# Batch 1 in eleven tiles of 512 tokens and one of 384, with part of the last tile's element work moved to PSUM and GpSimd

## The chip, the cores and the metric

One core of a Trainium2 chip runs the whole program. The metric is the device time of one execution in microseconds. The engines are called as in the profile: PE (TensorE) for matrix products, DVE (VectorE), ACT (ScalarE) and POOL (GpSimd) for element work, SP for issuing DMAs.

## The reference

Two batches of 6016 tokens with 256 channels pass through three layers, in float32:

```
qn, kn = q, k divided by their norms over the tokens
a  = softmax(kn^T qn / tau)            # 256 x 256 per batch
x  = v @ a                             # 12032 x 256
x  = (sigmoid(x @ w_gate) * (x @ w_val)) @ w_out        # inner width 1536
h  = x @ w_in ;  out = (h - tanh(h)) @ w_out2           # inner width 2048
```

## The kernel before, in words

Every product is made from float32 numbers split in two float32r halves, high and low: high by high, high by low and low by high are added in PSUM, so each product costs three matmuls (`prod`, lines 415 to 421). The attention matrix of a batch is multiplied into the gated layer's weights, after which only two layers are left: the gated layer (kind 1, 12 units per token tile) and the second layer (kind 2, 16 units per tile).

The tokens of a batch are cut into 12 tiles (`token_tiles`, line 46), of 502 tokens eight times and of 500 four times in either batch, so there are 24 tiles, numbered from 0. A unit runs in three parts. `part_a` makes the product in one or two PSUM buffers of a ring of four and starts the element work (`s1_a`, `s2_a`); `part_b`, one unit later, splits the result into halves (ACT copies the high half at line 489, DVE or POOL subtracts for the low half at line 491); `part_c`, three units later (`LAG`), multiplies the halves by the next weights and adds into two PSUM banks, `y0` and `y1` for kind 1, `o0` and `o1` for kind 2. At the last unit of a tile in kind 1 the banks `y` are split into `yhl`, on which the tile's second layer starts; at the last unit in kind 2 ACT copies the banks `o` out and issues the DMA. A gated unit has 18 matmuls (12 and 6), a unit of the second layer 12 (6 and 6), so a tile has 216 and 192.

The order is written out by hand: units are sorted by a key (lines 626 to 632), so that the second layer of tile i runs between the gated units of tile i+1, and every engine takes its instructions in program order. For the last tile (23) there is no next tile, and its 16 units of the second layer run alone at the end; the last units of tile 22 also fall after the last gated unit of tile 23.

Element work of a unit of the second layer (`s2_a`, lines 458 to 474) with H the product in PSUM: ACT makes u = H², d = tanh(H), s from u, and a mask `big` from u; DVE makes d = H - d (470), u = H·u (471), s = (s + C_D)·u (472), and replaces s by d where the mask is set (473). All of u, d, s and big lie in SBUF, two buffers each. In the units that `tail` names (tile 23, and units 12 to 15 of tile 22) the low half of line 491 is made by POOL, and s of odd units lies in another pool (`yp`).

Of the kernel before, what the change touches and what calls it, by code (L numbers as in the profile page):

```python
# [8 lines left out]
F32 = mybir.dt.float32  # L9
# [4 lines left out]
AF = mybir.ActivationFunctionType  # L14
ALU = mybir.AluOpType
AX = mybir.AxisListType

P = 128
B, S, D = 2, 6016, 256
# [3 lines left out]
K1, K2 = F1 // P, F2 // P  # L23
TPB = 12
CH = 512
NM = 502
NW = 12
NO = 6
NI = 8

# weight chunks converted before the second layer starts, steps of conversion between units, steps to wait for a
# conversion with two buffers, units between a product and its use, units over which batch 1's scores are spread
NC2 = 16
PUMP = 3
WAIT = 4
LAG = 3
SIDE0, SIDE1 = 2 * (K1 + K2), 10 * (K1 + K2)

# h - tanh(h) = h * u * r(u) with u = h * h; r(u) = (C_S u + C_B)^2 + C_D up to U_MAX
U_MAX = 0.045  # L40
C_S = 0.2293950247517065
C_B = -0.29057879500195016
C_D = 0.2488973


def token_tiles():
    out = []
    for b in range(B):
        off = 0
        for n in [NM] * 8 + [NM - 2] * 4:  # L50
            out.append((b, off, b * S + off, n))
            off += n
        assert off == S
    return out
# [3 lines left out]
def attn_moe_kernel(  # L58
# [12 lines left out]
    nc = tc.nc  # L71
# [15 lines left out]
    def bank(tag, name):  # L87
        return pp.tile([P, CH], F32, tag=tag, name=name)

# [1 line left out]
    def split(hi, lo, src):  # L91
        nc.scalar.copy(hi, src)
        nc.vector.tensor_sub(lo, src, hi.bitcast(F32))  # L93

    def convert(pool, items, second, done=None, depth=4):
        """float64 bit patterns to float32 halves hi + lo, two chunks side by side; stops after each Vector instruction"""
        jobs = {}

        def load(n):
            if n < len(items):  # L100
                src, dst, name = items[n]
                raw = pool.tile([P, CH, 2], U32, tag="craw", bufs=depth, name=f"raw_{name}")
                nc.sync.dma_start(raw, src.bitcast(U32).rearrange("p (c two) -> p c two", two=2))
                jobs[n] = [raw[:, :, 0], raw[:, :, 1], dst, name, None]

        def rebias(n):
            if n in jobs:
                x = pool.tile([P, CH], U32, tag="cx", bufs=depth, name=f"x_{jobs[n][3]}")
                nc.gpsimd.tensor_scalar_mul(x.bitcast(F32), jobs[n][1].bitcast(F32), 2.0**-112)
                jobs[n][4] = x  # L110

        def halves(n):
            if n in jobs:
                _, _, dst, _, x = jobs.pop(n)
                t = dst()
                nc.scalar.copy(t[:, 0], x.bitcast(F32))
                (nc.vector if second else nc.gpsimd).tensor_sub(t[:, 1], x.bitcast(F32), t[:, 0].bitcast(F32))
                if done is not None:
                    done(n)

        def step(n, which):
            if n not in jobs:
                return False
            w0, w1, _, _, x = jobs[n]
            if which == 0:
                nc.vector.tensor_scalar(x, x, 3, 0x7FFFFFFF, op0=ALU.logical_shift_left, op1=ALU.bitwise_and)
            elif which == 1:
                nc.vector.scalar_tensor_tensor(x, w1, 0x80000000, x, op0=ALU.bitwise_and, op1=ALU.bitwise_or)
            else:
                nc.vector.scalar_tensor_tensor(x, w0, 29, x, op0=ALU.logical_shift_right, op1=ALU.bitwise_or)  # L130
                load(n + depth)
            return True

        for n in range(depth):
            load(n)
        for n in range(2):
            rebias(n)
        yield
        for n in range(0, len(items) + 2, 2):
            if depth == 2 and n:  # L140
                for m in (n - 2, n - 1):
                    halves(m)
                for m in (n, n + 1):
                    rebias(m)
                for _ in range(WAIT):
                    yield
            for m in (n, n + 1):
                if step(m, 0):
                    yield
            if depth > 2:  # L150
                for m in (n - 2, n - 1):
                    halves(m)
                for m in (n + 2, n + 3):
                    rebias(m)
            for which in (1, 2):
                for m in (n, n + 1):
                    if step(m, which):
                        yield
# [5 lines left out]
            if stream[0] is not None and next(stream[0], 1) == 1:  # L164
                stream[0] = None

# [1 line left out]
    ident = base.tile([P, P], F32, name="ident")  # L168
    ident2 = sp.tile([P, 2, P], F32, name="ident2")
    ones = base.tile([P, P], F32, name="ones")  # L170
# [1 line left out]
    c_m = base.tile([P, 1], F32, name="c_m")  # L172
# [15 lines left out]
    def new_aw(f, b):  # L188
        return base.tile([P, 2, 2, CH], F32R, tag=f"aw{f}", name=f"aw{f}_{b}")

# [1 line left out]
    wgv_t = [wp.tile([P, 2, 2, CH], F32R, name=f"wgv{f}") for f in range(NW // 2)]  # L192
    conv = []
    for f in range(NW // 2):
# [59 lines left out]
        nc.scalar.activation(s0, n2, AF.Sqrt)  # L254

    def softmax_steps(pool, S_, e, rk, rq):
        """row softmax of S * rk * rq, left in e: scaled scores, exponentials, division, transpose"""
        mx = pool.tile([P, 6], F32, name="mx", tag="mx")

        def scores():  # L260
            for c in range(2):
                nc.vector.scalar_tensor_tensor(e[:, c], S_[:, c], rk[:, c : c + 1], rq, op0=ALU.mult, op1=ALU.mult)
            nc.vector.tensor_reduce(mx[:, 0:2], e, axis=AX.X, op=ALU.max)
            nc.vector.tensor_scalar_mul(mx[:, 0:2], mx[:, 0:2], -1.0)

        def exps():
            for c in range(2):
                nc.scalar.activation(e[:, c], e[:, c], AF.Exp, bias=mx[:, c : c + 1], accum_out=mx[:, 2 + c : 3 + c])

        def normalise():  # L270
            nc.vector.tensor_scalar_add(mx[:, 4:6], mx[:, 2:4], 1e-9)
            nc.vector.reciprocal(mx[:, 4:6], mx[:, 4:6])
            for c in range(2):
                nc.vector.tensor_scalar_mul(e[:, c], e[:, c], mx[:, 4 + c : 5 + c])

        def turn():
            ps = ring("turn").rearrange("p (j i) -> p j i", j=2)
            for jc in range(2):
                for ic in range(2):
                    nc.tensor.transpose(ps[:, jc, ic * P : (ic + 1) * P], e[:, ic, jc * P : (jc + 1) * P], ident)  # L280
            return ps

        return scores, exps, normalise, turn
# [10 lines left out]
    tiles = token_tiles()  # L294
    NT = len(tiles)
# [72 lines left out]
    scores, exps, normalise, turn = softmax_steps(sp, S0, e0, rn[:, 2:4], rqs)  # L368
# [39 lines left out]
        wi_t.append(w2p.tile([P, 2, CH], F32R, name=f"wi{c}"))  # L408
        wv_t.append(w2p.tile([P, 2, CH], F32R, name=f"wv{c}"))

# [1 line left out]
    yp = None  # L412
    yps, yhl, ops, live = {}, {}, {}, {}

# [37 lines left out]
        prod(ps, n, [pair(wi_t[m // 2], (m % 2) * 2 * P + j * P) for j in range(2)], [(h[:, 0, j, :n], h[:, 1, j, :n]) for j in range(2)])  # L452
        live[2, i, m] = ps

    def tail(i, m):
        return i == NT - 1 or (i == NT - 2 and m >= 12)

    def s2_a(i, m):
        n = tiles[i][3]
        H = live[2, i, m][:, :n]  # L460
        u = m2.tile([P, NM], F32, tag="u", bufs=2, name=f"u{i}_{m}")[:, :n]
        d = m2.tile([P, NM], F32, tag="d", bufs=2, name=f"d{i}_{m}")[:, :n]
        late = tail(i, m)
        s = (yp if late and m % 2 else m2).tile([P, NM], F32, tag="s", bufs=2, name=f"s{i}_{m}")[:, :n]
        big = m2.tile([P, NM], BF16, tag="big", bufs=2, name=f"big{i}_{m}")[:, :n]
        nc.scalar.activation(u, H, AF.Square)  # L466
        nc.scalar.activation(d, H, AF.Tanh)  # L467
        nc.scalar.activation(s, u, AF.Square, scale=C_S, bias=c_b[:, 0:1])  # L468
        nc.scalar.activation(big, u, AF.Relu, bias=c_m[:, 0:1])  # L469
        nc.vector.tensor_sub(d, H, d)  # L470
        nc.vector.tensor_mul(u, H, u)  # L471
        nc.vector.scalar_tensor_tensor(s, s, C_D, u, op0=ALU.add, op1=ALU.mult)  # L472
        nc.vector.copy_predicated(s, big.bitcast(I16), d)  # L473
        live[2, i, m] = s

# [8 lines left out]
    def part_b(u):  # L484
        _, kind, i, c = u
        n = tiles[i][3]
        hl = mp.tile([P, 2, NM], F32R, tag="hl", bufs=LAG + 1, name=f"hl{kind}_{i}_{c}")
        x = live[kind, i, c][:, :n]
        nc.scalar.copy(hl[:, 0, :n], x)  # L489
        eng = nc.gpsimd if kind == 2 and tail(i, c) else nc.vector  # L490
        eng.tensor_sub(hl[:, 1, :n], x, hl[:, 0, :n].bitcast(F32))  # L491
        live[kind, i, c] = hl

# [20 lines left out]
                    nc.scalar.copy(t[:, :n], ops[i][o][:, :n])  # L514
                    nc.scalar.dma_start(outT[o * P : (o + 1) * P, pos : pos + n], t[:, :n])

# [1 line left out]
    qp, qctx, q2ctx, q1 = None, ExitStack(), ExitStack(), {}  # L518

    def side_open():  # L520
# [101 lines left out]
    side += [lambda g=g: side_inverse(g) for g in range(4)]  # L622
    side += [lambda: q1["sm"][0](), lambda: q1["sm"][1](), lambda: q1["sm"][2](), side_turn, side_halves]

# [1 line left out]
    units = []  # L626
    for i in range(NT):
        for c in range(K1):
# [5 lines left out]
    qb, qc, after, awq = [], [], [], []  # L634
    m2 = None
# [88 lines left out]
```

## Time and profile before

| what | value |
|---|---|
| median of 3 runs | 2418.13 us (2416.43 to 2421.8) |
| profiled execution, from the first to the last instruction | 2414.9 us |
| what lies around that span, by the median and the ends of the runs | 3.2 us (1.5 to 6.9) |
| PE busy | 2376.3 us, 98% of the span |
| DVE busy | 1877.5 us, 78% |
| ACT busy | 1580.6 us, 65% |
| POOL busy | 113.9 us, 5% |
| mean granted TensorE clock | 0.994 of full speed |

The profiled execution has no time of its own beside its span, so the span is set against the runs. In the rows below a time with two decimals at the head of a line is the start in microseconds from the span's start, and the number after it how long the instruction took. Engines work pipelined, so that the next instruction on an engine can start before the one before it has ended; the distance from start to start is what an instruction costs its engine in a full queue.

### The profile page before, as it was taken

The page shows a single profiled execution, that of the slowest core. Times are in us where ns is not written, and L with a number is a line of the kernel's source. Part 1 is how long each engine was busy: PE and PEld are TensorE (multiplying, and loading weights), DVE is VectorE, ACT ScalarE, POOL GpSimd, SP SyncE. Part 2 cuts the span into 40 slices and gives each one's busy share as a digit, 9 for nine tenths or more (in the row PEclk, how much of TensorE's full clock was granted, in tenths as well). Part 3 has the DMA queues.
Part 4 walks back from the last instruction along what each step waited for, and adds up shares of the span by engine and source line. Part 5 has one row for each costly group of instructions (what it writes and reads, how often), then busy time and mean ns, then how long its engine had stood idle before and what let it go on. Part 6 is the DMA issues. An engine that isn't in the chain of part 4 may idle for free.

```text
span 2414.9 us, 28741 instructions
## 1 busy us (share of the span) xinstructions
PE 2376.3 (98%) x10704; PEld 1970.7 (82%) x10704; DVE 1877.5 (78%) x2911; ACT 1580.6 (65%) x2817; POOL 113.9 (5%) x79
## 2 busy tenths in 40 slices
PE   8899999999999999999999999999999999999998
PEld 8677888888888888878888888888888888888876
DVE  7898778887888888877777677777777777777778
ACT  4456667676766667776666666666666666666677
POOL 5530000000000000000000000000000000000003
PEclk9999999999999999999999999999999999999998
DMA  8520000100101101001110000000000000000000
GB/s 300 213 101 18 27 26 18 35 27 28 34 18 35 36 17 35 22 27 35 53 35 9 9 18 9 9 18 1 18 18 1 18 18 1 18 9 9 9 1 17
DMA packets 37516, 81.53 MB, mean 34 GB/s; under 512 B 3840, under 2 KB 28416, under 8 KB 35840
## 3 DMA queue, kind: packets, MB, share of 16 engines
q1 hardware_dynamic: 29568, 61.09, 7.8%
q10 hardware_dynamic: 6912, 12.32, 1.3%
q0 software_dynamic: 896, 6.29, 0.6%
q8 instruction: 83, 1.36, 0.2%
q14 instruction: 57, 0.47, 0.1%
HBM read 61.08 MB, written 18.61 MB: 33 GB/s over the span
## 4 chain that ended last, share of the span: by engine, by line
PE 92%; DVE 5%; ACT 1%; issue 1%; DMA 1%; POOL 0%; SPq 0%; ACTq 0%; POOLq 0%; DVEq 0%
PE ps L421 11%; PE ps L420 11%; PE ps L419 11%; PE o L420 7%; PE h L420 7%; PE h L419 7%; PE o L421 7%; PE o L419 7%; PE h L421 7%; PE y L420 5%; PE y L419 5%; PE y L421 5%; DVE s L472 1%; DVE u L471 1%; DVE s L473 1%
## 5 line engine op out<-in xcount | busy, mean ns | idle before, releaser
L470 DVE TENSOR_TENSOR d<-h,d 128x502 f32<-128x502 f32 (+1 forms) x384 | 259.7, 676 | 287.5 <-ACT d L467 287.4
L421 PE MATMUL ps<-vhl,aw 128*128 128x502 f32 (+1 forms) x1152 | 451.3, 392 | 0.0
L420 PE MATMUL ps<-vhl,aw 128*128 128x502 f32 (+1 forms) x1152 | 449.5, 390 | 0.7 <-DVE vhl L93 0.7
L419 PE MATMUL ps<-vhl,aw 128*128 128x502 f32 (+1 forms) x1152 | 449.7, 390 | 0.0
L489 ACT CAST hl<-s 128x502 fp32r<-128x502 f32 (+1 forms) x384 | 234.6, 611 | 290.1 <-DVE s L473 290.1
L466 ACT ACTIVATE u<-h 128x502 f32<-128x502 f32 (+1 forms) x384 | 226.8, 591 | 296.9 <-PE h L421 296.5
L471 DVE TENSOR_TENSOR u<-h,u 128x502 f32<-128x502 f32 (+1 forms) x384 | 259.5, 676 | 114.6 <-ACT big L469 114.3
L420 PE MATMUL o<-hl,wv 128*128 128x502 f32 (+1 forms) x768 | 303.3, 395 | 7.6 <-POOL hl L491 4.3
L419 PE MATMUL o<-hl,wv 128*128 128x502 f32 (+1 forms) x768 | 300.7, 392 | 3.6 <-ACT out L514 1.8
L420 PE MATMUL h<-yhl,wi 128*128 128x502 f32 (+1 forms) x768 | 300.5, 391 | 2.4 <-DVE yhl L93 2.4
L419 PE MATMUL h<-yhl,wi 128*128 128x502 f32 (+1 forms) x768 | 300.8, 392 | 0.0
L421 PE MATMUL o<-hl,wv 128*128 128x502 f32 (+1 forms) x768 | 300.0, 391 | 0.0
L421 PE MATMUL h<-yhl,wi 128*128 128x502 f32 (+1 forms) x768 | 298.7, 389 | 0.0
L473 DVE COPY_PREDICATED s<-big,d 128x502 f32<-128x502 int16 (+1 forms) x384 | 284.4, 741 | 13.3
L472 DVE SCALAR_TENSOR_TENSOR s<-s,u 128x502 f32<-128x502 f32 (+1 forms) x384 | 274.3, 714 | 14.4
L468 ACT ACTIVATE s<-u,c_b 128x502 f32<-128x502 f32 (+1 forms) x384 | 275.2, 717 | 0.0
L469 ACT ACTIVATE big<-u,c_m 128x502 bf16<-128x502 f32 (+1 forms) x384 | 273.3, 712 | 0.0
L420 PEld LDWEIGHTS ps<-vhl,aw 128*128 128x128 f32 x1152 | 218.0, 189 | 46.4 <-DVE vhl L93 1.1
L419 PEld LDWEIGHTS ps<-vhl,aw 128*128 128x128 f32 x1152 | 217.3, 189 | 45.3 <-DVE aw L93 0.4
L421 PEld LDWEIGHTS ps<-vhl,aw 128*128 128x128 f32 x1152 | 216.9, 188 | 44.2
L443 DVE TENSOR_TENSOR sg<-ps,sg 128x502 f32<-128x502 f32 (+1 forms) x288 | 194.2, 674 | 69.0 <-PE ps L421 67.5
L442 ACT ACTIVATE sg<-ps 128x502 f32<-128x502 f32 (+1 forms) x288 | 170.3, 591 | 114.4 <-PE ps L421 103.4
(143 smaller groups left out, 3765.8 us busy)
## 6 DMA issues: line engine op xcount, KB each, us to landing
vraw<-in_vT_dram SPq DMA_DIRECT2D x16, 502.0 KB, 3.7
out_dram<-out ACTq DMA_DIRECT2D x32, 251.0 KB, 2.0
raw<-in_q_dram SPq DMA_DIRECT2D x48, 128.0 KB, 2.1
raw<-in_k_dram SPq DMA_DIRECT2D x48, 128.0 KB, 2.2
raw_wgv<-in_wgv_dram SPq DMA_DIRECT2D x12, 512.0 KB, 6.5
wgv_d<-wgv POOLq DMA_DIRECT2D x6, 1024.0 KB, 9.0
wb<-wgv_d SPq DMA_DIRECT2D x6, 1024.0 KB, 4.8
raw<-in_q_dram SPq DMA_DIRECT2D x11, 512.0 KB, 5.3
```

Source lines behind the costliest of these rows:

```text
L419: mm(ps[:, :n], wh, xh, start=first and j == 0, stop=False)
L420: mm(ps[:, :n], wh, xl, start=False, stop=False)
L421: mm(ps[:, :n], wl, xh, start=False, stop=last and j == m - 1)
L443: nc.vector.tensor_mul(sg[:, :n], V[:, :n], sg[:, :n])
L466: nc.scalar.activation(u, H, AF.Square)
L468: nc.scalar.activation(s, u, AF.Square, scale=C_S, bias=c_b[:, 0:1])
L469: nc.scalar.activation(big, u, AF.Relu, bias=c_m[:, 0:1])
L470: nc.vector.tensor_sub(d, H, d)
L471: nc.vector.tensor_mul(u, H, u)
L472: nc.vector.scalar_tensor_tensor(s, s, C_D, u, op0=ALU.add, op1=ALU.mult)
L473: nc.vector.copy_predicated(s, big.bitcast(I16), d)
L489: nc.scalar.copy(hl[:, 0, :n], x)
```

## The change

Batch 1 is cut into eleven tiles of 512 tokens and one of 384; batch 0 stays as it was. `NM`, the width of the buffers in SBUF, goes from 502 to 512. In the last tile H·u no longer overwrites u but goes to the PSUM bank `y0` or `y1` (as w), which the gated layer no longer needs, and line 472 reads it there. In odd units of the last tile the mask is made by GpSimd in place of ACT. The low halves of units 12 to 15 of tile 22, which GpSimd made, go back to DVE, and their s to the common pool.

```diff
-NM = 502
+NM = 512
...
-        for n in [NM] * 8 + [NM - 2] * 4:
+        for n in [502] * 8 + [500] * 4 if b == 0 else [NM] * 11 + [S - 11 * NM]:
...
-    def tail(i, m):
-        return i == NT - 1 or (i == NT - 2 and m >= 12)
...
-        late = tail(i, m)
-        s = (yp if late and m % 2 else m2).tile([P, NM], F32, tag="s", bufs=2, name=f"s{i}_{m}")[:, :n]
+        s = (yp if i == NT - 1 and m % 2 else m2).tile([P, NM], F32, tag="s", bufs=2, name=f"s{i}_{m}")[:, :n]
...
+        last = i == NT - 1
+        w = bank(f"y{m % 2}", f"w{m}")[:, :n] if last else u
...
-        nc.scalar.activation(big, u, AF.Relu, bias=c_m[:, 0:1])
+        if last and m % 2:
+            nc.gpsimd.tensor_scalar(big, u, U_MAX, 1.0, op0=ALU.is_gt, op1=ALU.mult)
+        else:
+            nc.scalar.activation(big, u, AF.Relu, bias=c_m[:, 0:1])
         nc.vector.tensor_sub(d, H, d)
-        nc.vector.tensor_mul(u, H, u)
-        nc.vector.scalar_tensor_tensor(s, s, C_D, u, op0=ALU.add, op1=ALU.mult)
+        nc.vector.tensor_mul(w, H, u)
+        nc.vector.scalar_tensor_tensor(s, s, C_D, w, op0=ALU.add, op1=ALU.mult)
...
-        eng = nc.gpsimd if kind == 2 and tail(i, c) else nc.vector
+        eng = nc.gpsimd if kind == 2 and i == NT - 1 else nc.vector
```

## Rows read from the trace of the kernel before

**Rows 1.** The page: busy time by engine, and the chain that ended last.

```profile
PE 2376.3 (98%) x10704; PEld 1970.7 (82%) x10704; DVE 1877.5 (78%) x2911; ACT 1580.6 (65%) x2817; POOL 113.9 (5%) x79
...
PE 92%; DVE 5%; ACT 1%; issue 1%; DMA 1%; POOL 0%; SPq 0%; ACTq 0%; POOLq 0%; DVEq 0%
```

**Rows 2.** Busy time by stretch; columns: stretch, length, each engine's busy time, PEclk, DMA.

```profile
1400.00:1600.00 200.00, 200.00 (x878) 165.40 (x877) 149.28 (x232) 131.13 (x235) 0.00 (x0) 1.00 0.04 11
...
2000.00:2200.00 200.00, 200.00 (x881) 165.65 (x880) 149.73 (x234) 130.29 (x235) 0.00 (x0) 1.00 0.03 11
...
2350.00:2380.00 30.00, 27.79 (x113) 21.88 (x112) 27.97 (x35) 25.20 (x46) 10.16 (x8) 0.94 0.05 18
2380.00:2400.00 20.00, 17.84 (x74) 12.93 (x72) 19.17 (x25) 16.64 (x30) 7.59 (x6) 1.00 0.00 0
2400.00:2415.00 15.00, 8.98 (x20) 5.25 (x18) 6.50 (x9) 5.14 (x9) 3.74 (x3) 0.56 0.09 34
```

**Rows 3.** Timeline of DVE: tile 22's last unit and the start of tile 23.

```profile
2349.26 0.66 DVE L471 TENSOR_TENSOR u<-h,u 128x500 f32<-128x500 f32 x1
2349.96 0.68 DVE L472 SCALAR_TENSOR_TENSOR s<-s,u 128x500 f32<-128x500 f32 x1
2350.67 0.74 DVE L473 COPY_PREDICATED s<-big,d 128x500 f32<-128x500 int16 x1
2351.30 0.67 DVE L470 TENSOR_TENSOR d<-h,d 128x500 f32<-128x500 f32 x1
```

**Rows 4.** Timeline of all engines: tile 23's last unit and the end.

```profile
2402.74 0.72 DVE L473 COPY_PREDICATED s<-big,d 128x500 f32<-128x500 int16 x1
...
2403.35 0.66 DVE L470 TENSOR_TENSOR d<-h,d 128x500 f32<-128x500 f32 x1
2403.49 0.61 ACT L489 CAST hl<-s 128x500 fp32r<-128x500 f32 x1 [0.54 <-DVE s L473]
...
2403.93 0.67 DVE L471 TENSOR_TENSOR u<-h,u 128x500 f32<-128x500 f32 x1
...
2404.23 1.25 POOL L491 TENSOR_TENSOR hl<-s,hl 128x500 fp32r<-128x500 f32 x1 [2.07 <-ACT hl L489]
...
2404.70 1.31 DVE L472 SCALAR_TENSOR_TENSOR s<-s,u 128x500 f32<-128x500 f32 x1
...
2406.05 0.72 DVE L473 COPY_PREDICATED s<-big,d 128x500 f32<-128x500 int16 x1
...
2408.85 0.79 PE L420 MATMUL o<-hl,wv 128*128 128x500 f32 x1 [0.44 <-POOL hl L491]
```

**Rows 5.** Groups by line on DVE from 2352 us to the end.

```profile
L472 DVE SCALAR_TENSOR_TENSOR s<-s,u 128x500 f32<-128x500 f32 x16 | 22.0, 1376 | 1.7
```

**Rows 6.** Timeline of PE: first and last of twelve 512-column groups, with the start behind each.

```profile
1133.12 0.39 PE L289 MATMUL aw<-wb,aT 128*128 128x512 f32 x1
...
1134.50 0.38 PE L419 MATMUL h<-yhl,wi 128*128 128x500 f32 x1
...
1228.82 0.39 PE L289 MATMUL aw<-wb,aT 128*128 128x512 f32 x1
...
1230.20 0.39 PE L419 MATMUL ps<-vhl,aw 128*128 128x502 f32 x1
```

**Rows 7.** Timeline of PE: first and last of six matmuls of 256 columns.

```profile
451.41 0.28 PE L223 MATMUL qk<-hl 128*128 128x256 f32 x1
...
452.00 0.28 PE L225 MATMUL qk<-hl 128*128 128x256 f32 x1
```

**Rows 8.** Timeline of PE at the start of tile 23's second layer.

```profile
2348.23 0.49 PE L420 MATMUL h<-yhl,wi 128*128 128x500 f32 x1 [2.22 <-DVE yhl L93]
```

**Rows 9.** Line 109 on POOL: one undisturbed pass; then durations in ns, min/median/max.

```profile
163.25 1.54 POOL L109 TENSOR_SCALAR x_wv<-raw_wv 128x512 f32<-128x512 f32 x1
...
L109 POOL TENSOR_SCALAR x_wo<-raw_wo x6: 1507/1732/3113, 94.0 to 109.4; 128x512 f32<-128x512 f32 x6
```

## The prediction, made before the change was run

> **What bounds the kernel now.** I read the page's shares first: PE is busy 98% of the span, and the chain that ended last lies on PE for 92% of it and on DVE for 5% [rows 1]. Then the stretches: in two long stretches of batch 1 PE is never idle, DVE is busy three quarters of the time and ACT two thirds; near the end, at 2380 to 2400 us, PE drops to 89% while DVE is at 96% [rows 2]. So there are two regimes, and the change touches both. In the long one only PE's matmuls count. In the end, where tile 23's second layer runs alone, DVE sets the pace, and the timeline shows with what. A unit that nothing disturbs costs DVE 0.70 for line 471 (2349.26 to 2349.96), 0.71 for 472, 0.63 for 473 [rows 3] and 0.58 for 470 (2403.35 to 2403.93 [rows 4]): 2.62 us. But units come 3.34 us apart there: line 472 takes 1.31 us in place of 0.68, and 1376 ns in the mean of the last 16 [rows 5]. The reason is in rows 4. POOL makes the low half of the unit before from 2404.23 to 2405.48; line 472, which reads s and u, both in SBUF, starts at 2404.70 and ends 0.53 after POOL. It waited. Lines 470 and 471 read one operand from PSUM, and 471 took its usual 0.67 although POOL began inside it. The wait closes a loop: 473 ends, ACT copies the high half, POOL subtracts, 472 waits for POOL, 473 follows.
>
> **Term 1, PE's long stretch.** Tiles, instructions and total columns stay; what moves is which columns lie in the long stretch. Start to start, a matmul of 502 columns costs 200/878 = 0.2278 us and one of 500 200/881 = 0.2270 [rows 2]; one of 256 costs 0.59/5 = 0.118 [rows 7]. The line through 256 and 500 has 0.447 ns a column: 0.1752 at 384 and 0.2324 at 512. But the trace has 512-column matmuls among PE's full queue: twelve groups of six, 1.38 us in the first and in the last, 0.2300 each [rows 6]. I take 0.231, between the two. Gated layer of batch 1 (216 matmuls a tile): 216 x (8 x 0.2278 + 4 x 0.2270) = 589.8 before, 216 x (11 x 0.231 + 0.1752) = 586.7 after: -3.1. Second layer of tiles 12 to 22 (192 a tile): 192 x (8 x 0.2278 + 3 x 0.2270) = 480.7 before, 192 x 11 x 0.231 = 487.9 after: +7.2, since 116 columns leave the last tile for the tiles ahead of it. Together **+4.1**; with 0.2300 it is -0.4, with 0.2324 +10.3. DVE and ACT grow in step with PE there and stay hidden. Wider buffers, input loads and output DMAs in batch 1 cost nothing under PE's full queue; the DMA share there is 0.03 to 0.04 [rows 2].
>
> **Term 2, the passage to tile 23.** PE idles 2.22 us there, waiting for `yhl` [rows 8], and DVE is the late one. Three low halves of tile 22 go back from POOL to DVE ahead of it or right behind, 3 x 0.58 = +1.7; two waits of line 472 there go away, each at most 0.63 (1.31 - 0.68 [rows 4]), some -1.0; wider units of tile 22 add 0.2. **+1.0**, with 0 (hidden by PE's queue) and +2 as ends. The same columns sit in `s` of the common pool with two buffers; DVE runs these units in order, so nothing new waits.
>
> **Term 3, the 16 units of tile 23.** Line 470's 0.58 us for 500 columns is at most 1.16 ns a column, so 116 columns are worth 0.13 us at most; I take 0.12 for each of the four: 0.46 for 470, 0.58 for 471, 0.59 for 472, 0.51 for 473, together 2.14 us a unit. PE needs 12 x 0.1752 = 2.10. ACT was busy 16.64 of 20 us, 2.78 a unit of 3.34 [rows 2]; by 384/500 that is 2.1, and it loses every other mask. So DVE would set the pace at 2.14, with PE right behind, if POOL disturbed nothing. Line 472 now has one operand in PSUM, as 471 had, and I take it that it no longer waits. What about 473? It reads `big` and `d`, both in SBUF. No row has it beside a busy POOL; between "does not wait", like 471, and "waits", like 472, its operands are those of 472, so I take that it waits.
>
> Walk from the start of a 473 at 0. ACT's copy starts at 0.63 (0.75 before: 2402.74 to 2403.49), POOL's subtraction at 1.25 (0.74 later before, now 0.62), and lasts 0.97 (1.25 x 384/500, rounded up), to 2.22 [rows 4]. DVE would reach the next 473 at 2.14 and waits until 2.22. The mask of the odd unit after that is queued on POOL behind this subtraction. Its price has no row: the nearest is a one-input POOL pass at 512 columns, 1.54 us undisturbed [rows 9], by columns 1.16; ends are near 0 and 3.11, the longest such pass. The waiting 473 runs first (0.51), then the mask (1.16), then the next subtraction (0.97), and the 473 after that has waited for all: 2.64. A pair costs 2.22 + 2.64 = 4.86, a unit 2.43. From the first line 470 of tile 23 (2351.30 [rows 3]) to its last (2403.35 [rows 4]) are 15 intervals, 52.05 us, of which 15 x 3.34 = 50.1 is the pace and 2.0 the start and the copying out of tile 22. After: 15 x 2.43 + 1.5 = 38.0. **-14.1**. Behind the mask only POOL's subtraction is queued, and behind that the `o` products on PE.
>
> The Trainium skill (SBUF — State Buffer, Who interferes with whom) says that a DVE instruction with two SBUF inputs and a GpSimd instruction that reads SBUF exclude each other; that agrees with the 1.31 us of line 472, and by it 473 would wait for the mask too, which speaks against this half of the change. The Trainium skill (GPSIMD Engine Reference, Performance versus the Vector engine) gives 769 ns for a tight one-input loop over 512 elements, half of the 1.54 us in the row; by that page the mask would be an estimated 0.58, the pair 2.22 + 2.14, and the sum about -14.5.
>
> **Term 4, the end.** From the last line 470 to the end were 11.5 us (2403.35 to 2414.9). Lines 470 to 472 took 2.70 and now 1.63 plus some 0.5 of waiting; behind the last 473, the 2.80 us up to PE's product with the low half (2406.05 to 2408.85) shrink by 23%, 0.65, and I allow 0.5 for the products and copies behind it. **-1.7** (-1 to -2.3). The output DMA stays.
>
> **Sum:** 4.1 + 1.0 - 14.1 - 1.7 = -10.7 us. The span goes from 2414.9 to 2404.2; the median of the runs lies 3.2 above the span, so 2407.4.
>
> PE's clock: it was granted 1.00 at 2380 to 2400 with PE 89% busy, and 0.56, partly the lower level, behind 2400 where only `o` products were left [rows 2]. At 2.1 of 2.43 us PE stays as busy as before, so I cost this at nothing; if it fell to the lower level within tile 23, 12 matmuls would take about 4 us, and PE would be the bound.
>
> **The rivals.**
> (a) 473 does not wait. Then the unit is 2.14 us, term 3 is 15 x 2.14 + 1.5 - 52.05 = -18.45 and term 4 -2.3: -15.6, **2402.5**. For it: line 471 ran beside a busy POOL undisturbed. Against: 473's operands.
> (b) The PSUM operand does not free 472, so that part of the change does nothing. 472 would come at 0.51 + 0.46 + 0.58 = 1.55 and wait until 2.22, 473 follows at 2.81: 15 x 2.81 + 1.5 - 52.05 = -8.4, sum -5.0, **2413.1**. Line 471 speaks against it.
> (c) A mask of 2.33 us (3.11 by columns): second interval 0.51 + 2.33 + 0.97 = 3.81, 3.02 a unit, sum about -1.9, **2416.2**: no difference that can be told.
> (d) The other side, one mechanism: GpSimd's mask is slow whatever its width, and 473 waits for it. At 3.11 the second interval is 4.59, the unit 3.41, term 3 +0.5, sum +3.9, **2422.0**. It decides from a mask of 2.6 us on, where the sum is 0, and shows as slower from 3.2. For it: a comparison with two constants and a bf16 output has no row on POOL. Against: the undisturbed passes take 1.54 at a greater width.
>
> **How the numbers follow.** The forecast gets 0.45, (a) 0.30, (b) 0.08, (c) 0.09, (d) 0.08. 0.2% is 4.8 us, about what a measurement of this kernel can tell from no change. The forecast with the upper end of term 1 is still -4.5, (a) is faster throughout, (b) for half of its ends: faster 0.78, within 0.2% 0.15, slower 0.07 (the upper part of (d), since nothing caps an operation without a row). The range takes the forecast with both ends of term 1 (2402.9 to 2413.6) and (b), (a) down to 2400, and reaches to the edge of (c): 2400 to 2416.
>
> **What would show it.** Line 472 in tile 23 near 0.56 us beside a busy POOL; 473 stretched where POOL works; intervals of 470 alternating near 2.2 and 2.6; the mask near 1.2 us; 512-column matmuls at 0.230 to 0.232 start to start; first line 470 of tile 23 some 5 us later than 2351.30. A mask beyond 2.6 us, a 472 that still lasts over 1 us, or PE at the lower clock within tile 23 would make it wrong.

## The result, and the profile after

The changed kernel takes 2373.14 us (median of 4 runs, 2371.08 to 2378.72) against 2418.07: a ratio of 0.9818, with a 95% interval of 0.9803 to 0.9833. That is 45 us, four times the 10.7 forecast, and below the range. The profiled execution is the slowest of the four (2378.72, span 2376.9; the other spans are 2369.3 to 2372.6), so the rows below show 38 of the 45 us.

The lines of the changed kernel stand one further down: 470 to 473 of before are 471 to 474, 491 is 492; 468 is GpSimd's mask. The page first, busy time by engine and the chain that ended last, against [rows 1]:

```profile
PE 2335.7 (98%) x10704; PEld 1959.8 (82%) x10704; DVE 1874.0 (79%) x2915; ACT 1564.9 (66%) x2809; POOL 118.9 (5%) x83
...
PE 91%; DVE 5%; ACT 1%; issue 1%; DMA 1%; POOL 0%; ACTq 0%; POOLq 0%; DVEq 0%; SPq 0%
```

The picture is the same, still 10704 matmuls and still 98%, but PE is busy for 41 us less (2376.3 to 2335.7). Stretches of the kernel after (stretch, length, busy time of PE, PEld, DVE, ACT, POOL with counts, clock, DMA), one in batch 0, two in batch 1, one in tile 23's second layer:

```profile
400.00:600.00 200.00, 200.00 (x934) 169.38 (x933) 168.63 (x266) 139.82 (x255) 0.00 (x0) 1.00 0.10 29
...
1400.00:1600.00 200.00, 200.00 (x884) 165.62 (x883) 152.72 (x233) 131.15 (x235) 0.00 (x0) 1.00 0.04 14
...
2000.00:2200.00 200.00, 200.00 (x884) 165.62 (x883) 151.35 (x232) 132.40 (x237) 0.00 (x0) 1.00 0.03 11
...
2327.00:2368.00 41.00, 36.37 (x190) 32.49 (x188) 36.69 (x64) 32.99 (x72) 28.29 (x22) 1.00 0.04 13
```

and the two of the kernel before that were not shown:

```profile
400.00:600.00 200.00, 200.00 (x916) 167.02 (x915) 164.96 (x260) 138.56 (x251) 0.00 (x0) 1.00 0.09 28
...
2351.30:2403.40 52.10, 46.31 (x183) 34.93 (x182) 49.13 (x62) 43.32 (x79) 18.99 (x15) 0.95 0.03 10
```

Two things were not forecast. In batch 1, 200 us hold 884 matmuls of 512 columns where they held 878 to 881 narrower ones [rows 2]: 0.2262 each, where 0.231 was taken. And batch 0, whose tiles did not change, fits 934 where it fitted 916. The granted clock is 1.00 in all of these long stretches, before and after, so it is not the clock. PE's timeline after, first and last of 27 matmuls in a row, against [rows 6]:

```profile
1499.91 0.39 PE L419 MATMUL ps<-vhl,aw 128*128 128x512 f32 x1
...
1505.81 0.39 PE L421 MATMUL o<-hl,wv 128*128 128x512 f32 x1
```

26 steps in 5.90 us are 0.2269. Tile 23's second layer on DVE, its passage from tile 22, against [rows 3]:

```profile
2326.63 0.68 DVE L492 TENSOR_TENSOR hl<-s,hl 128x512 fp32r<-128x512 f32 x1
2327.22 0.55 DVE L471 TENSOR_TENSOR d<-h,d 128x384 f32<-128x384 f32 x1
2327.69 0.55 DVE L472 TENSOR_TENSOR w<-h,u 128x384 f32<-128x384 f32 x1
2328.35 0.56 DVE L473 SCALAR_TENSOR_TENSOR s<-s,w 128x384 f32<-128x384 f32 x1
2329.01 0.60 DVE L474 COPY_PREDICATED s<-big,d 128x384 f32<-128x384 int16 x1
```

The low half of line 492 is DVE's again, as the diff has it. The first line 471 of tile 23 comes at 2327.22, 24 us earlier than its like before and not 5 later. PE idles there 0.88 and 1.93 us, against 2.22 in one piece [rows 8]:

```profile
2321.23 0.45 PE L419 MATMUL h<-yhl,wi 128*128 128x384 f32 x1 [0.88 <-ACT yhl L92]
2323.61 0.54 PE L420 MATMUL h<-yhl,wi 128*128 128x384 f32 x1 [1.93 <-DVE yhl L93]
```

A settled pair of units after, DVE and POOL of the timeline of all engines (ACT and PE left out but for one copy), against [rows 4]; the first line is the one mask that found nothing in its way, to be set beside [rows 9]:

```profile
2336.23 1.50 POOL L468 TENSOR_SCALAR big<-u 128x384 bf16<-128x384 f32 x1 [1.51 <-ACT u L464]
...
2345.04 1.02 POOL L492 TENSOR_TENSOR hl<-s,hl 128x384 fp32r<-128x384 f32 x1 [1.08 <-ACT hl L490]
...
2345.42 0.55 DVE L473 SCALAR_TENSOR_TENSOR s<-s,w 128x384 f32<-128x384 f32 x1
...
2346.08 0.60 DVE L474 COPY_PREDICATED s<-big,d 128x384 f32<-128x384 int16 x1
2346.14 1.85 POOL L468 TENSOR_SCALAR big<-u 128x384 bf16<-128x384 f32 x1
...
2348.07 1.00 POOL L492 TENSOR_TENSOR hl<-s,hl 128x384 fp32r<-128x384 f32 x1
...
2348.35 1.18 DVE L474 COPY_PREDICATED s<-big,d 128x384 f32<-128x384 int16 x1
```

Line 473 (472 of before) starts inside POOL's subtraction and takes 0.55: with its operand in PSUM it no longer waits. Line 474 (473 of before) does: 1.18, and it ends 0.46 after POOL, where the one before took 0.60. The subtraction it waits for was late because the mask stood ahead of it on POOL. This is the loop that the prediction walked. Groups by line on DVE in this part, against [rows 5]:

```profile
L474 DVE COPY_PREDICATED s<-big,d 128x384 f32<-128x384 int16 x16 | 14.0, 877 | 1.6
L473 DVE SCALAR_TENSOR_TENSOR s<-s,w 128x384 f32<-128x384 f32 x16 | 8.9, 555 | 1.7
```

Cut into legs at three instructions, the profiled executions compare so (us; e1, e12 and e8 are experiments below):

| leg | before | after | e1 | e12 | e8 |
|---|---|---|---|---|---|
| start to the split of `vhl` of tile 12 | 1222.3 | 1213.4 | 1205.1 | 1207.0 | 1206.1 |
| from there to the first d = H - d of tile 23 | 1129.0 | 1113.8 | 1107.5 | 1112.4 | 1113.8 |
| fifteen units, to the last d = H - d | 52.05 | 39.81 | 52.73 | 43.67 | 36.79 |
| to the end | 11.5 | 9.9 | 11.3 | 9.8 | 9.0 |

The two ends went nearly as forecast. What was missed lies in the first two legs, 24 us of this execution and some 6 more of the others. In the first leg e1, e12 and e8, which have the same batch 0, are 6 to 8 us ahead of this execution, and the traces show where it lost them. From 197.6 to 335.5 us its 591 products stand 233.3 ns apart, whatever their kind; then come six matmuls of 256 columns, and behind them the products take 223.8. In e1, e12 and e8 they take 223.3 there already. So the stretch from 200 to 400 us holds fewer matmuls after (the first line) than before (the second), with PE busy throughout and the clock at 1.00 in both:

```profile
200.00:400.00 200.00, 200.00 (x885) 166.22 (x884) 154.27 (x242) 135.29 (x243) 0.00 (x0) 1.00 0.06 19
...
200.00:400.00 200.00, 200.00 (x893) 166.05 (x892) 156.16 (x245) 135.51 (x245) 0.00 (x0) 1.00 0.07 20
```

591 products times 9.9 ns are 5.9 us. What brings PE into this slower rhythm is open.

### The profile page after: what moved, and what is told of

Same layout as the page of the kernel before. It is cut to its first block, busy times and chain, and to the rows that moved or that the text cites. A ratio compares the mean times of both kernels' runs of the same rounds, so it can differ in the third digit from the quotient of the medians.

```text
span 2376.9 us, 28760 instructions
## 1 busy us (share of the span) xinstructions
PE 2335.7 (98%) x10704; PEld 1959.8 (82%) x10704; DVE 1874.0 (79%) x2915; ACT 1564.9 (66%) x2809; POOL 118.9 (5%) x83
## 4 chain that ended last, share of the span: by engine, by line
PE 91%; DVE 5%; ACT 1%; issue 1%; DMA 1%; POOL 0%; ACTq 0%; POOLq 0%; DVEq 0%; SPq 0%
PE ps L420 11%; PE ps L419 11%; PE ps L421 11%; PE o L420 7%; PE o L421 7%; PE o L419 7%; PE h L420 7%; PE h L421 7%; PE h L419 7%; PE y L421 5%; PE y L419 5%; PE y L420 5%; DVE s L473 1%; DVE s L474 1%; DMA raw<-in_k_dram 0%
## 5 line engine op out<-in xcount | busy, mean ns | idle before, releaser
L471 DVE TENSOR_TENSOR d<-h,d 128x512 f32<-128x512 f32 (+3 forms) x384 | 260.4, 678 | 260.4 <-ACT d L465 260.3
L420 PE MATMUL ps<-vhl,aw 128*128 128x512 f32 (+3 forms) x1152 | 444.9, 386 | 0.7 <-DVE vhl L93 0.7
L419 PE MATMUL ps<-vhl,aw 128*128 128x512 f32 (+3 forms) x1152 | 445.2, 386 | 0.0
L421 PE MATMUL ps<-vhl,aw 128*128 128x512 f32 (+3 forms) x1152 | 444.6, 386 | 0.0
L472 DVE TENSOR_TENSOR u<-h,u 128x512 f32<-128x512 f32 (+2 forms) x368 | 251.4, 683 | 112.2 <-ACT big L470 111.8
L420 PE MATMUL o<-hl,wv 128*128 128x512 f32 (+3 forms) x768 | 299.3, 390 | 9.1 <-POOL hl L492 5.8
L474 DVE COPY_PREDICATED s<-big,d 128x512 f32<-128x512 int16 (+3 forms) x384 | 289.1, 753 | 14.3
L419 PE MATMUL o<-hl,wv 128*128 128x512 f32 (+3 forms) x768 | 298.0, 388 | 2.0 <-ACT hl L490 1.2
L420 PE MATMUL h<-yhl,wi 128*128 128x512 f32 (+3 forms) x768 | 297.2, 387 | 2.1 <-DVE yhl L93 2.1
L419 PE MATMUL h<-yhl,wi 128*128 128x512 f32 (+3 forms) x768 | 296.9, 387 | 0.9 <-ACT yhl L92 0.9
L421 PE MATMUL o<-hl,wv 128*128 128x512 f32 (+3 forms) x768 | 297.7, 388 | 0.0
L421 PE MATMUL h<-yhl,wi 128*128 128x512 f32 (+3 forms) x768 | 297.0, 387 | 0.0
L466 ACT ACTIVATE s<-u,c_b 128x512 f32<-128x512 f32 (+3 forms) x384 | 275.1, 716 | 3.5 <-DVE hl L492 3.5
L470 ACT ACTIVATE big<-u,c_m 128x512 bf16<-128x512 f32 (+3 forms) x376 | 268.4, 714 | 0.0
L473 DVE SCALAR_TENSOR_TENSOR s<-s,u 128x512 f32<-128x512 f32 (+2 forms) x368 | 253.1, 688 | 12.6
L492 DVE TENSOR_TENSOR hl<-s,hl 128x512 fp32r<-128x512 f32 (+2 forms) x368 | 248.4, 675 | 0.0
```

The costliest lines, as they stand in the source:

```text
L419: mm(ps[:, :n], wh, xh, start=first and j == 0, stop=False)
L420: mm(ps[:, :n], wh, xl, start=False, stop=False)
L421: mm(ps[:, :n], wl, xh, start=False, stop=last and j == m - 1)
L472: nc.vector.tensor_mul(w, H, u)
L473: nc.vector.scalar_tensor_tensor(s, s, C_D, w, op0=ALU.add, op1=ALU.mult)
```

## The experiments

All kernels compute the whole reference; they differ in tiles, buffers, padding and in who makes what. Times are medians of 4 runs (10 for e2, e3, e4 and e6) beside runs of the kernel before on the same chip (2416.9 to 2418.2). "Pitch" is the mean distance from one matmul's start to the next in the trace, over all products of a kind and width in batch 1 (1230 to 2240 us). The kinds by moving operand and weight: ps is `vhl` by `aw`, y is `hl` by `wo`, h is `yhl` by `wi`, o is `hl` by `wv`.

**e1_buffers512: the buffers alone.** The kernel before with wider buffers and nothing else.

```diff
-NM = 502
+NM = 512
...
-        for n in [NM] * 8 + [NM - 2] * 4:
+        for n in [502] * 8 + [500] * 4:
```

> The kernel before with its own tiles of 502 and 500 tokens and its own tail; only the buffers in SBUF are 512 columns wide, so that the halves of vhl, yhl and hl lie 2048 bytes apart in place of 2008. Layout theory (where a moving half starts in SBUF sets what a matmul costs): all 502- and 500-column matmuls fall from 0.228 and 0.227 us start to start to about 0.225 and 0.2245, as batch 0 of the changed kernel shows, 9800 matmuls by 2.8 ns: 25 to 33 us faster, about 2388. Width theory (only matmuls of 512 columns are cheap, the fall in batch 0 is chance): 0 to 6 us faster, 2412 to 2418.

2379.91 us, ratio 0.9844 [0.9828, 0.986]: **38 of the 45 us**, with the same 24 tiles, the same instructions and the old tail, more than the 25 to 33 that the layout theory gave. Stretches of e1 (columns as above), one in batch 0 and one in batch 1:

```profile
400.00:600.00 200.00, 200.00 (x936) 169.48 (x935) 167.00 (x264) 140.68 (x256) 0.00 (x0) 1.00 0.10 30
...
1400.00:1600.00 200.00, 200.00 (x897) 167.99 (x896) 147.99 (x230) 130.52 (x237) 0.00 (x0) 1.00 0.04 14
```

897 in place of 878: the pitch of 502 columns, 227.4 to 228.5 by kind, became 223.3 to 223.4. The program has 24 x 408 = 9792 products of all four kinds and either width. Over both batches their mean pitch fell by 4.2 ns (227.8 to 223.7 between 230 and 2240 us), and 9792 x 4.2 ns is 41 us.

**e2_skew514 and e3_buffers504: is it width or a particular width?** e2 is the kernel after with `NM = 514` and its own tiles; e3 the kernel before with `NM = 504` and its own tiles.

```diff
-NM = 512
+NM = 514
...
-        for n in [502] * 8 + [500] * 4 if b == 0 else [NM] * 11 + [S - 11 * NM]:
+        for n in [502] * 8 + [500] * 4 if b == 0 else [512] * 11 + [384]:
```

```diff
-NM = 502
+NM = 504
...
-        for n in [NM] * 8 + [NM - 2] * 4:
+        for n in [502] * 8 + [500] * 4:
```

> The changed kernel with its own tiles of 512 and 384; only the buffers are 514 columns wide, so that the halves lie 2056 bytes apart. Layout theory: 512-column matmuls go from 0.2267 back to 0.230 to 0.231, and 502 to 0.228: 18 us in batch 1 and 12 to 15 in batch 0, about 2405. Width theory: within 5 us of the changed kernel, 2371 to 2378.

> The kernel before with buffers 504 columns wide: halves 2016 bytes apart, a multiple of 32 but not of 64 bytes. Layout theory at 32 bytes: as with 512-wide buffers, about 2388. Layout theory at 64 bytes or more: half of the halves still start askew, a gain of half that or less, 2400 to 2418. Width theory: 2418.

e2: 2413.68, ratio 0.9982 [0.9973, 0.9992]; e3: 2413.08, 0.998 [0.997, 0.9989]. The change with buffers two columns wider than its own brings some 4 us: it lost more than the layout theory said (about 2405). A stretch of e2 with 512-column matmuls:

```profile
1400.00:1600.00 200.00, 200.00 (x863) 162.22 (x862) 148.45 (x227) 131.94 (x233) 0.00 (x0) 1.00 0.03 11
```

863 against 884 after: 0.2317, where the prediction had 0.231. So its durations were those of the old kind of layout, and the layout is the thing that moved.

**e4_hl_only, e5_halves512, e6_rest512: which buffers?** The kernel before (tiles and element code) with 512 columns for `hl` alone (e4), for `vhl`, `yhl` and `hl` (e5), or for all others but these (e6, which is e1 with 502 in the three).

```diff
-        hl = mp.tile([P, 2, NM], F32R, tag="hl", bufs=LAG + 1, name=f"hl{kind}_{i}_{c}")
+        hl = mp.tile([P, 2, 512], F32R, tag="hl", bufs=LAG + 1, name=f"hl{kind}_{i}_{c}")
...
-        h = vp.tile([P, 2, 2, NM], F32R, tag="vhl", name=f"vhl{i}")
+        h = vp.tile([P, 2, 2, 512], F32R, tag="vhl", name=f"vhl{i}")
...
-                h = pool.tile([P, 2, 2, NM], F32R, tag="yhl", name=f"yhl{i}")
+                h = pool.tile([P, 2, 2, 512], F32R, tag="yhl", name=f"yhl{i}")
```

The first pair is e4, all three are e5.

> The kernel before, where only the buffer hl (moving operand of the y and o matmuls, 168 of the 408 matmuls of a tile) is 512 columns wide. If a matmul pays for the start of its own operand: y and o fall by some 2.5 ns, ps and h stay, 10 to 12 us faster, about 2407. If the cost comes from elsewhere in the layout (the writes of DVE and ACT, or the matmuls' phase against each other): all kinds move alike, or none.

> The kernel before where the three buffers that PE reads as moving operands (vhl, yhl, hl) are 512 columns wide, so that all halves start 32 bytes past a multiple of 64; the buffers of the element work (u, d, s, sg, big, out) and of the input stay at 502. Own-read theory (PE pays for the starts of its moving operands, and one askew kind spoils the others, which is why hl alone brought nothing): all kinds at 0.2235 to 0.2255, 33 to 40 us faster, about 2380. Contention theory (PE's reads collide with askew accesses of ACT and DVE): no kind below 0.227, within 6 us of 2418.

> The reverse: only the buffers of the element work and of the input are 512 wide, vhl, yhl and hl stay at 502. Own-read theory: within 6 us of 2418. Contention theory: the gain of the run with all buffers at 512, about 2380.

e4 2422.2 (1.0016 [1.0006, 1.0025]), e5 2403.73 (0.9947 [0.993, 0.9963]), e6 2419.73 (1.0009 [1.0, 1.0018]). None of the parts gives the whole: with `hl` at 512 even the products that read it stayed at 228, and e5 lies between the two forecasts made for it. So width was the wrong quantity to vary; what differs as well is where the buffers lie. In e1 and in the kernel after, `vhl`, `yhl`, `hl`, both halves of each (2048 bytes apart), and all weights begin at a byte address of the partition that leaves 224 when divided by 256; before, the halves are 2008 bytes apart and scattered, and in e5 they begin at 160, 160 and 96, against weights at 224.

**e10_shift32: e1 with 32 bytes of padding** ahead of `sg`, of `hl`, of the element buffers and of the second `yhl`.

```diff
+    mp.tile([P, 8], F32, name="pad1")
...
+        if (kind, i, c) == (1, 0, 0):
+            mp.tile([P, 8], F32, name="pad2")
...
+                yp.tile([P, 8], F32, name="pad4")
...
+            m2.tile([P, 8], F32, name="pad3")
```

> The kernel before with all buffers 512 columns wide, where pads of 32 bytes put the buffers of the element work (sg, u, d, s, big, out) at a multiple of 64 while vhl, yhl and hl stay 32 bytes past one. If the element buffers must have the same place within 64 bytes as PE's operands: the gain of the 512-wide element buffers goes, 0.2265 and more start to start, about 2400 to 2404. If it is enough that each buffer's parts lie alike, or the place does not matter: 2380.

2404.11 (0.9947 [0.993, 0.9963]); y and o rose to 228, h to 225, ps stayed at 224. It looked like contention with the element buffers. That reading did not hold: the pads lay ahead of other buffers too, so `hl` had moved by 64 bytes and the second `yhl` by 128. Four more runs take these apart.

**e13 to e16: e1 with one group moved.** e13 moves `vhl`, `yhl`, `hl`, `aw`, `wo` and the element buffers by 32 bytes, but not `wi` and `wv`; e14 the element buffers alone, by 32; e15 `hl` by 64 bytes, e16 by 128, and in both `u`, `d`, `s`, `big` and `out`, which lie behind `hl`, move with it.

```diff
+    base.tile([P, 8], F32, name="pad0")
```

is e13, ahead of `wo`; e15 has the following, and e16 the same with 32 columns in either pad; e14 has pads of 8 columns ahead of `sg` and `u` and of 56 behind, so that `hl` and `yhl` keep their place.

```diff
+        if (kind, i, c) == (1, 0, 0):
+            mp.tile([P, 16], F32, name="pad2")
...
+                yp.tile([P, 48], F32, name="pad4")
```

> The tiles of 502 and 500 with buffers 512 wide (as in e1_buffers512, 2379.9 us), with 32 bytes of padding ahead of everything but the last two weights: all halves (vhl, yhl, hl), two weights (aw, wo) and the element buffers begin at 0 instead of 224 modulo 256; wi and wv, which the products of h and of o read as stationary operands, stay at 224. If what counts is that all moving operands begin at one and the same phase: 502-token products stay at about 224 ns, total 2375 to 2385 us. If the moving operand has to agree with the weight it is multiplied with: ps (weights aw) and y (wo) stay at 224, h and o rise to about 228, total 2393 to 2404 us. If phase 224 itself is the good one: all four at about 228, total 2413 to 2420 us.

> As e1_buffers512, with the element buffers (sg, u, d, s and the large ones) moved by 32 bytes, to 0 modulo 256, while every half and every weight stays at 224. If only the start of the moving operands counts: all products at about 224 ns, 2376 to 2384 us. If it is how the element buffers that the other engines read and write at the same time lie against the halves: y and o at about 228 ns as in e10_shift32, 2398 to 2408 us.

> As e1_buffers512, with hl moved by 64 bytes, to 32 modulo 256 (u, d and s come to 32 too), vhl and yhl left at 224. If the own start of the moving operand counts: the products y and o, which read hl, at about 228 ns, ps and h at 224, 2398 to 2408 us (as e10_shift32 gave, where the element buffers had moved as well). If it was the element buffers in e10_shift32: all at 224, 2376 to 2384 us.

> As e1_buffers512, with hl moved by 128 bytes, to 96 modulo 256 and thus to the same place modulo 128 as before. If a place modulo 128 (or 64 or 32) is what counts: all products at about 224 ns, 2376 to 2384 us. If modulo 256: y and o at 226.5 to 228 ns, 2390 to 2408 us.

**e17_w_shift and e18_all_192: the counter-proof.** In e17 no moving operand moves, only the weights `wi` and `wv`, by 32 bytes; in e18 everything goes to a new common place.

The first line, behind the tiles of `wi` and `wv`, is in both, the second in e18 alone.

```diff
+    w2p.tile([P, 8], F32, name="pad5")
...
+    base.tile([P, 56], F32, name="pad0")
```

> As e1_buffers512, with only the weights wi and wv moved by 32 bytes, to 192 modulo 256; every half, aw, wo and the element buffers stay at 224. No moving operand moves. If what counts is that a moving operand and the weight it is multiplied with begin at the same place modulo 256: h (yhl by wi) and o (hl by wv) at about 228 ns, ps (vhl by aw) and y (hl by wo) at about 224, total 2396 to 2408 us. If the moving operand's own place decides: all at 224, 2376 to 2384 us.

> As e1_buffers512, with every half, all four weights and the element buffers moved to 192 modulo 256. If only the agreement of moving operand and weight counts: all products at 223.5 to 225 ns, total 2376 to 2388 us. If 224 modulo 256 is a good place by itself: all at about 228 ns, 2413 to 2420 us.

Distance in bytes, modulo 256, between the start of a moving operand and that of its weight (for e5 of the first `yhl` buffer, the second is at 128), and pitch of the 502-column products of batch 1:

| run | median us | ps: distance, ns | y | h | o |
|---|---|---|---|---|---|
| e1 | 2379.9 | 0, 223.4 | 0, 223.4 | 0, 223.4 | 0, 223.3 |
| e18 | 2379.4 | 0, 223.4 | 0, 223.4 | 0, 223.4 | 0, 223.3 |
| e14 | 2380.0 | 0, 223.4 | 0, 223.5 | 0, 223.4 | 0, 223.3 |
| e13 | 2403.7 | 0, 224.4 | 0, 225.7 | 32, 227.9 | 32, 227.8 |
| e17 | 2404.2 | 0, 224.4 | 0, 225.7 | 32, 227.9 | 32, 227.8 |
| e15 | 2403.7 | 0, 224.2 | 64, 228.2 | 0, 224.2 | 64, 228.2 |
| e16 | 2398.1 | 0, 223.5 | 128, 227.6 | 0, 224.4 | 128, 227.2 |
| e5 | 2403.7 | 64, 227.1 | 128, 226.5 | 64, 227.4 | 128, 226.7 |

In e17 one and the same `hl` is multiplied with `wo`, in its old place, and with `wv`, moved by 32 bytes. PE's timeline of e17, six products h, six products o, and later six products y (its lines 420 to 422 are 419 to 421 of the kernel before):

```profile
1500.30 0.38 PE L420 MATMUL h<-yhl,wi 128*128 128x502 f32 x1
...
1501.67 0.39 PE L420 MATMUL o<-hl,wv 128*128 128x502 f32 x1
...
1503.04 0.39 PE L420 MATMUL ps<-vhl,aw 128*128 128x502 f32 x1
...
1505.72 0.39 PE L420 MATMUL y<-hl,wo 128*128 128x502 f32 x1
...
1507.06 0.38 PE L420 MATMUL ps<-vhl,aw 128*128 128x502 f32 x1
```

Six h take 1.37 us, six o 1.37, six y 1.34. And e18, all at 192, is as fast as e1. A stretch of e18:

```profile
1400.00:1600.00 200.00, 200.00 (x897) 168.01 (x896) 147.77 (x231) 130.54 (x238) 0.00 (x0) 1.00 0.04 14
```

and the same stretch of e17, 11 matmuls fewer:

```profile
1400.00:1600.00 200.00, 200.00 (x886) 166.87 (x885) 150.42 (x234) 133.32 (x239) 0.00 (x0) 1.00 0.04 14
```

So neither the place of the moving operand (e17 leaves it) nor a particular place (e18) nor the element buffers (e14) make the difference between these runs, but **whether a moving operand and its weight begin at the same place modulo 256 bytes**. Modulo 128 is not enough (e16), and modulo 512 is not needed: in e1 h and o lie 256 bytes apart modulo 512, ps and y 0, and all four take the same.

The rule is not the whole of it. The 591 products at 233.3 ns in the kernel after agree with their weights too. Kinds that agree lose 1 to 2 ns in e13 and e17 when others disagree, and their 500-column products up to 3 (ps 226.8 in e15, 223.6 in e1). In e15 that loss of the 502-column products lies at the seam: the first h or ps behind a y or o takes 228.8 to 229.8 ns (221.2 to 222.5 in e1), those inside a row of their own kind 223.4 to 223.7. And in e5 the 500-column ps had 221.7, the lowest of all.

**e12_old_tail: the tiles without the tail's edits.** The kernel after, with the element code of the kernel before, which is the kernel before with these lines:

```diff
-NM = 502
+NM = 512
...
-        for n in [NM] * 8 + [NM - 2] * 4:
+        for n in [502] * 8 + [500] * 4 if b == 0 else [NM] * 11 + [S - 11 * NM]:
```

> The changed kernel's tiles and 512-wide buffers with the whole end of the kernel before: H times u over u in SBUF, every mask on ACT, low halves of tile 22's last four units on POOL. Theory: line 472 waits for POOL again and units of 384 come 2.8 us apart (1.55 after a 473, then 0.67 of waiting), 15 x (2.8 - 2.56) = 3 to 4 us and 1 more at the passage: 2374 to 2379. Rival that all of the gain at the end is the edits and none the width of 384: 14 us slower than the changed kernel, 2387.

2374.32 (0.9822 [0.9807, 0.9836]), 1.2 us above the changed kernel and inside its interval. Line 472 waits as it did, and a settled unit takes 2.74 us. Its group on DVE:

```profile
L472 DVE SCALAR_TENSOR_TENSOR s<-s,u 128x384 f32<-128x384 f32 x14 | 15.6, 1112 | 1.5
```

In the table of legs e12 against e1 is what the tiles alone do: +4.8 us in the second leg, -9.1 in tile 23's units, -1.5 behind. The first leg has +1.9 more, but nothing differs there, and 1.7 of it is there at the first split of `vhl` already (83.2 against 81.5 us).

**e9_w_sbuf and e8_act_mask: the two halves of the tail's edit.** e9 puts w in SBUF, e8 gives all masks back to ACT.

The first edit is e9, the second e8.

```diff
-        w = bank(f"y{m % 2}", f"w{m}")[:, :n] if last else u
+        w = mp.tile([P, NM], F32, tag="sg", bufs=2, name=f"w{m}")[:, :n] if last else u
```

```diff
-        if last and m % 2:
+        if False:
```

> The changed kernel with w of the last tile in the SBUF buffers of sg in place of PSUM; the mask of odd units stays on GpSimd. Theory that the PSUM operand is what frees line 473 from POOL: 473 lasts 1.1 us and more where POOL works, the interval of units goes from 2.56 to 2.8 or 3.1 in the mean, 4 to 8 us slower than the changed kernel, 2377 to 2381. Rival that the narrower tile alone freed it: 473 stays at 0.56, no difference, 2373.

> The changed kernel with every mask on ACT, as before; w stays in PSUM. In the changed kernel's trace the pairs of units of tile 23 take 5.12 us, 2.26 and 2.86, and the mask lasts 1.85. Theory that line 474 waits for the mask on POOL: without it every interval is 2.26 or PE's and ACT's 2.1 to 2.2, 15 x 0.3 = 4 to 5 us faster than the changed kernel, about 2368.5. Rival that ACT without the masks is what gave the short intervals: 2 to 5 us slower, about 2377.

e9: 2375.53 (0.9834 [0.9818, 0.985]), between its two forecasts, so the trace decides: units of 2.75 and 2.88, fifteen in 43.26 where the kernel after takes 39.81. Groups on DVE in e9, where 473 waits again and 474 hardly does:

```profile
L473 DVE SCALAR_TENSOR_TENSOR s<-s,w 128x384 f32<-128x384 f32 x13 | 13.1, 1010 | 1.4
L474 DVE COPY_PREDICATED s<-big,d 128x384 f32<-128x384 int16 x14 | 9.7, 694 | 1.4
```

e8: 2367.40 (0.9797 [0.9782, 0.9811]); every settled unit 2.27, fifteen in 36.79. The same lines in e8, neither waiting long:

```profile
L474 DVE COPY_PREDICATED s<-big,d 128x384 f32<-128x384 int16 x16 | 10.5, 653 | 1.7
...
L473 DVE SCALAR_TENSOR_TENSOR s<-s,w 128x384 f32<-128x384 f32 x16 | 8.9, 555 | 1.7
```

Without the mask the tail's edits are worth 6.9 us in the fifteen units (43.67 in e12, 36.79 in e8), and without the PSUM operand 0.4 (43.26 in e9). GpSimd's mask gives 39.81 - 36.79 = 3.0 us away in the units and 0.9 behind them.

**e7_both and e11_both_act: better versions.** e7 cuts batch 0 as batch 1; e11 does that too and takes e8's mask.

```diff
-        for n in [502] * 8 + [500] * 4 if b == 0 else [NM] * 11 + [S - 11 * NM]:
+        for n in [NM] * 11 + [S - 11 * NM]:
```

> The changed kernel with both batches in eleven tiles of 512 and one of 384. With 0.2267 for 512 columns, 0.1752 for 384, and 0.2252 and 0.2245 for 502 and 500 as batch 0 of the changed kernel shows, batch 0 goes from 408 x (8 x 0.2252 + 4 x 0.2245) = 1101.4 to 408 x (11 x 0.2267 + 0.1752) = 1088.9: 12 us faster than the changed kernel, about 2361. If the fixed part of a matmul does not matter (cost in step with columns): no difference, 2373.

> Both batches in eleven tiles of 512 and one of 384, and every mask on ACT; w in PSUM. The two single runs gave 2367.4 each against 2373.1 for the changed kernel; if they add, 2361 to 2363. If the saving in batch 0 and the one at the end are the same time (the clock, or run-to-run phase): 2367.

e7 2367.43 (0.9796 [0.9782, 0.9811]); e11 **2362.86** (0.9775 [0.976, 0.9789]), the fastest of all, 10 us below the kernel after. e7 gained half of the 12 us forecast for it, against the kernel after: the forecast took 0.2252 and 0.2245 us for batch 0 from the one profiled execution, which had the 233.3 ns in it. With 0.2234 and 0.2237, as in e1, the same sum gives some 5. In e11 the 512-column products have a pitch of 226.7 to 226.9, so a column costs 0.443 ns, against 223.4/502 = 0.445 in e1.

## Why the prediction was wrong, by its own steps

**The step that failed** is the sentence in Term 1 that wider buffers cost nothing under PE's full queue. It asked what the wider buffers cost on queues that PE hides; it did not ask what they do to PE itself. They changed how moving operands and weights lie to each other, and every large product fell by some 4 ns: -38.2 us (e1), where 0 was put and no rival stood. The pitches of [rows 2, 6] were taken as a function of the columns alone; 0.231 for 512 is right in the old kind of layout (0.2317 in e2) and 0.2267 in the new one. With -38.2 the sum would have been -48.9; measured were -45.

**Term 1's arithmetic** held: from the split of tile 12 to tile 23's units the tiles alone cost +4.8 (e12 against e1), forecast +4.1. The start of those units itself is 6.8 later, but the other 1.9 lie in batch 0, where nothing differs. With the durations of the new layout (0.2234, 0.2237, 0.2267 and 0.1749 us for 502, 500, 512 and 384 columns) the same sum gives +3.9, since all of them fell together.

**Term 2**, +1.0: from the split of tile 12 to the first d of tile 23 the new tail takes 1.4 more than the old (1113.8 against 1112.4).

**Term 3**, -14.1, came out at -12.2. The mechanism was the one walked: 473 freed, 474 waiting for the subtraction (the prediction's 472 and 473), intervals alternating, at 2.26 and 2.86 where 2.22 and 2.64 were forecast. The mask was mis-sized: 1.50 undisturbed and 1.85 with the wait for 474, taken as 1.16 from [rows 9] by columns. So the settled pace is 2.56 and not 2.43, 1.9 us in fifteen. Most of the term is the narrower tile (-9.1, e12); the edits add -3.9, and without the mask they would add -6.9 (e8).

The Trainium skill (SBUF — State Buffer, Who interferes with whom) says that a DVE instruction with two SBUF inputs contends with a GpSimd instruction that reads SBUF, and one with at most one SBUF input, outside the two-port modes, does not. The traces agree: line 474 took 1.18 where it started behind POOL's subtraction and 0.60 where it started ahead of the mask, and for line 473 the mean is 1.01 with w in SBUF (e9) and 0.56 with w in PSUM. The Trainium skill (GPSIMD Engine Reference, Performance versus the Vector engine) gives 769 ns over 512 elements as the best case of a tight loop; the mask, at 1.50 us for 384 columns, is far from it, and the measurement decides.

**Term 4**, -1.7: measured -1.6.

**The rivals.** (a) falls: 474 waits, and 2.27 a unit needs a POOL without masks (e8). (b) falls by e9, (c) and (d) by the mask's 1.50 to 1.98 us. The clock was 1.00 from 2327.2 to 2366 us, as assumed for the settled units; at the start of tile 23's second layer it was at the lower level (0.50) for 3.4 us, from 2323.8, behind 3.8 us in which PE was busy for 1.0. The kernel before had 3.4 us of 0.50 too, from 2360.9. All rivals were about the tail, some 15 us in all, while PE's part, 92% of the chain [rows 1], got one term with a spread of 11 us. Batch 0, whose tiles don't change (the 916 that became 934), was not even in the sum.

## What to carry to other kernels

Where PE is the bound, the buffers' addresses belong to the cost of its matmuls: before a duration of the old kernel is used for a new one, see whether the change moves a matmul's operands, and try a layout in which moving operands and weights begin at the same place modulo 256 bytes (halves of 2048 bytes did it here, since everything ahead of them left the same remainder). Test a buffer's width apart from the tiles that use it, since one constant can hold the whole gain. A DVE instruction that waited for GpSimd was freed here by moving one of its inputs to PSUM, but the next one with both inputs in SBUF then took over the wait, and new work on GpSimd in the same loop made that wait longer. Look at more than one execution: the profiled one had 6 us of slower matmuls that other traces of the same batch 0 don't show.

## What the runs showed of the hardware that was not expected

The pitch of a float32r matmul in a full queue depends here on the relation of two addresses: 223.4 ns for 502 columns where moving operand and weight begin at the same place modulo 256 bytes, 226.5 to 228.2 where they are 32, 64 or 128 bytes apart, at the same granted clock of 1.00. Moving the weight alone does it (e17, +4.5 ns for h and o). Weights are loaded beside the running matmul (the PEld rows overlap PE), so that the two reads meet somewhere is a possible reason, which no run here shows. The Trainium skill (SBUF — State Buffer, Who interferes with whom) lists TensorE's read ports for the moving operand and for the weights as independent; by that alone nothing in e17 should have changed, and it cost 24 us. Where all agree the kinds also come out alike: 226.7 for 512 columns in every kind after, against 231.4 to 232.9 in e2. And one layout can run in two rhythms: at agreeing addresses the kernel after held 233.3 ns for 138 us of batch 0, until six matmuls of 256 columns came between, and e1 for 17 us from 160.8 us on, until a matmul waited; behind that both took 223 to 224.
